# TensorE's K loop gets an empty first turn, and the MLP and q's products run at its end

## The chip, the cores and the metric

The kernel runs on one core of a Trainium2 chip. The metric is the device time of one execution in microseconds, the median of several runs. Four compute engines matter here: TensorE (PE, with PEld for its weight loads), VectorE (DVE), ScalarE (ACT) and GpSimd (POOL). SyncE (SP) issues nearly all DMAs, in the order of one queue.

## The reference

One decode step: sliding-window attention over a KV cache, an MLP with a shifting step, and their sum.

```python
def _A_ref(x, k_cache, v_cache, wq, wo):      # x (4,1,576), caches (4,16,8192,128)
    q = (x @ wq) ...                           # 32 heads of 128, two per KV head
    k = jnp.repeat(k_cache[:, :, Sk - W:, :], rep, axis=1)     # W = 2048
    v = jnp.repeat(v_cache[:, :, Sk - W:, :], rep, axis=1)
    p = _softmax(einsum("bhqd,bhkd->bhqk", q, k) * Dh ** -0.5)
    return einsum("bhqk,bhkd->bhqd", p, v) ... @ wo
def _B_ref(x, w1, w2, w3, w4):                 # 576 -> 576 -> 576 -> 4608 -> 576
    h = _gelu(_layernorm(x) @ w1)
    x1 = x + shifted(h) @ w2
    return x1 + _gelu(_layernorm(x1) @ w3) @ w4
xn = _layernorm(x)
return x + _A_ref(xn, ...) + _B_ref(xn, ...)
```

All data are bf16. The cache windows are 33.6 MB of K and as much of V; with the weights 88.49 MB are read from HBM.

## The kernel before

**Loads.** SP issues in this order: w1, w2, wq, w3, K load 0 in two halves, K loads 1 to 7, V loads 0 to 7 (the last in two halves), w4, wo in five pieces. A K or V load is 4,096 KB. K rotates through three slots (`kslot`), so from load 3 on a K load waits for the end of the transposes of the load three before it (`t_done`, semaphore `T`). K load 1 waits for q's products, K load 2 and the first V load for the products with w3. V loads 1 to 3 wait for transposes of the last K loads, V loads from 4 on for PV products, w4 and wo for later ones. Since all of these stand in one queue of issues, a waiting issue holds back those behind it.

**TensorE's prologue** (`prog["pe"]`, put out by `emit_program("pe", "pe", e)`). It runs before the loop: a zeroing product into q's bank, transposes of the normalised x (L328), nine products with w1 (L389), eighteen with w2 (L397), transposes of the third layer norm's output, 36 products with wq (L361), four transposes of q, two zeroing products, 72 products with w3 (L422), 18 products that transpose the MLP's hidden state (L435), and a wait for `Qs0`, the copy of q into the score groups' weights. In all 175 matmuls, each with its weight load.

**TensorE's K loop** (`nc.Fori`, L654). Eight turns, one for each K load, TensorE alone; the other engines have their programs unrolled. One turn has two halves `h`. A half transposes 64 blocks of 128x128 (`emit_T`, L474, into four PSUM banks in rotation), then multiplies one score group of 32 matmuls (`emit_SC`, L481) from the half before. The transposed blocks are evicted into `ktb` by VectorE (L462, five of eight) and ScalarE (L461, three of eight). Since the slot of a K load has to be a constant in the code, each half has three arms (`half(h, 0)`, `half(h, 1)`, `half(h, 2)`) and a register, `k_at`, chooses among them (L669 to L674). `turn` is the value that the loop's semaphore waits compare with: 1 in the first turn, 8 in the last.

**After it.** The last score group, softmax, a second loop for the PV products (L551), then the products with w4 and wo into one PSUM bank, and the result's DMA.

The order in which TensorE's instructions lie in memory is that of the code: prologue (361 instructions with the weight loads), loop (923), the rest (981).

## Time and profile before

| | |
|---|---|
| median of 3 runs | 219.47 us (218.48 to 220.06) |
| profiled execution | 218.1 us |
| its span, first to last instruction | 216.8 us |
| mean granted TensorE clock | 0.937 |
| PE busy | 179.4 us (83%) |
| DVE, ACT, POOL busy | 118.2, 61.5, 13.8 us |
| data read from HBM | 88.49 MB, 408 GB/s over the span |

How to read it: a busy TensorE is not one at its peak, as matmuls are pipelined and their ends are modelled. The DMA share says how much of the time the 16 DMA engines had packets, not how fast these went; the rate stands beside it. "Issue" as the reason of an idle time means that the engine waited for nothing that the profile shows. Branches and register steps of a sequencer are not counted as busy; they show up in the view of one source line.

### The profile page before, as it was taken

The page shows a single profiled execution, that of the slowest core. Times are in us where ns is not written, and L with a number is a line of the kernel's source. Part 1 is how long each engine was busy: PE and PEld are TensorE (multiplying, and loading weights), DVE is VectorE, ACT ScalarE, POOL GpSimd, SP SyncE. Part 2 cuts the span into 40 slices and gives each one's busy share as a digit, 9 for nine tenths or more (in the row PEclk, how much of TensorE's full clock was granted, in tenths as well). Part 3 has the DMA queues.
Part 4 walks back from the last instruction along what each step waited for, and adds up shares of the span by engine and source line. Part 5 has one row for each costly group of instructions (what it writes and reads, how often), then busy time and mean ns, then how long its engine had stood idle before and what let it go on. Part 6 is the DMA issues. An engine that isn't in the chain of part 4 may idle for free.

```text
span 216.8 us, 5426 instructions
## 1 busy us (share of the span) xinstructions
PE 179.4 (83%) x2459; PEld 144.3 (67%) x2459; DVE 118.2 (55%) x170; ACT 61.5 (28%) x69; POOL 13.8 (6%) x29
## 2 busy tenths in 40 slices
PE   1466254675999999999999996699999899999875
PEld 0222123655898888888888884489888698887442
DVE  5434201322677777787878784999966566401100
ACT  2003101131466656566555576400000000000000
POOL 8960000000000000000000000000000000000000
PEclk9995558767999999999999999999999999999999
DMA  7999899999999999999999999999999999999992
GB/s 268 413 435 490 367 428 423 426 475 393 404 423 378 399 387 405 411 435 387 441 431 429 441 417 447 423 438 357 411 426 435 435 426 411 459 445 429 388 414 106
DMA packets 4059, 88.66 MB, mean 409 GB/s; under 512 B 456, under 2 KB 592, under 8 KB 1104
## 3 DMA queue, kind: packets, MB, share of 16 engines
q1 hardware_dynamic: 4032, 88.49, 96.8%
q8 instruction: 9, 0.15, 0.3%
q14 instruction: 2, 0.02, 0.0%
q10 hardware_dynamic: 16, 0.01, 0.0%
HBM read 88.49 MB, written 0.00 MB: 408 GB/s over the span
## 4 chain that ended last, share of the span: by engine, by line
PE 61%; DMA 25%; DVE 5%; issue 5%; ACT 1%; SPq 1%; DVEq 0%
PE ps L474 27%; PE ps L551 20%; DMA vring<-in_A_wo_dram 13%; DMA vring<-in_B_w_dram 13%; PE ps L481 10%; PE ps L422 2%; SPq L200 1%; DVE rm L497 1%; DVE vring L494 1%; DVE ktb L543 1%; PE ps L511 1%; DVE ktb L462 1%; ACT Qpad L503 1%; ACT kring L527 1%; PE ps L562 0%
## 5 line engine op out<-in xcount | busy, mean ns | idle before, releaser
L461 ACT ACTIVATE ktb<-ps 128x1024 bf16<-128x1024 bf16 x48 | 49.3, 1027 | 45.4 <-PE ps L474 45.4
L462 DVE COPY ktb<-ps 128x1024 bf16<-128x1024 bf16 x80 | 52.1, 687 | 17.6 <-PE ps L474 16.6
L474 PE MATMUL ps<-ident_bf,kring 128*128 128x128 bf16 x768 | 49.1, 228 | 9.2 <-issue 8.6
L474 PEld LDWEIGHTS ps<-ident_bf,kring 128*128 128x128 bf16 x768 | 46.6, 102 | 13.2 <-issue 12.6
L543 DVE TENSOR_TENSOR ktb<-kring,mH_bf 128x4096 bf16<-128x4096 bf16 x16 | 36.2, 2290 | 10.1 <-PE ps L551 9.9
L551 PE MATMUL ps<-vring,ktb 128*128 128x256 bf16 x256 | 28.6, 273 | 3.0 <-DVE ktb L543 1.9
L551 PEld LDWEIGHTS ps<-vring,ktb 128*128 128x128 bf16 x256 | 24.9, 98 | 6.3 <-issue 3.5
L551 PE MATMUL ps<-kring,ktb 128*128 128x256 bf16 x256 | 28.6, 273 | 0.0
L551 PEld LDWEIGHTS ps<-kring,ktb 128*128 128x128 bf16 x256 | 25.0, 98 | 3.3
L481 PE MATMUL ps<-ktb,kring 128*32 128x256 bf16 x544 | 23.4, 315 | 0.1
L609 ACT ACTIVATE out_sb<-ps 4x288 bf16<-4x288 f32 x1 | 0.4, 399 | 75.8 <-PE ps L384 75.8
L481 PEld LDWEIGHTS ps<-ktb,kring 128*32 128x32 bf16 x544 | 14.3, 101 | 5.3 <-issue 0.8
L474 PE MATMUL ps<-ident_bf,vring 128*128 128x128 bf16 x256 | 15.2, 219 | 0.1
L474 PEld LDWEIGHTS ps<-ident_bf,vring 128*128 128x128 bf16 x256 | 14.3, 98 | 1.4 <-issue 1.1
L422 PE MATMUL ps<-vring,xs 128*8 128x320 bf16 (+1 forms) x72 | 4.5, 429 | 5.7 <-DMA vring<-in_B_w_dram 5.7
L492 DVE COPY vring<-ps 128x256 f32<-128x256 f32 x8 | 4.8, 605 | 7.4 <-PE ps L481 7.4
L494 DVE TENSOR_TENSOR vring<-vring,ps 128x256 f32<-128x256 f32 x8 | 5.4, 680 | 6.2 <-PE ps L481 6.2
L572 DVE TENSOR_SCALAR tmp<-ps,maskd 128x128 f32<-128x128 f32 x2 | 0.7, 352 | 13.7 <-PE ps L551 13.7
L328 PE MATMUL ps<-ident_bf,xp_bf 4*128 4x4 bf16 x15 | 0.8, 164 | 8.2 <-DVE xp_bf L312 5.0
L422 PEld LDWEIGHTS ps<-vring,xs 128*8 128x8 bf16 x72 | 2.1, 111 | 8.1 <-DMA vring<-in_B_w_dram 6.3
L610 DVE CAST out_sb<-ps 4x288 bf16<-4x288 f32 x1 | 0.4, 449 | 12.9 <-PE ps L384 12.9
L239 POOL MEMSET ktb<- 128x8192 bf16 x1 | 6.9, 6924 | 0.0
(93 smaller groups left out, 92.0 us busy)
## 6 DMA issues: line engine op xcount, KB each, us to landing
kring<-in_A_k_cache_dram SPq DMA_DIRECT2D x5, 4096.0 KB, 14.7
vring<-in_A_v_cache_dram SPq DMA_DIRECT2D x4, 4096.0 KB, 20.6
kring<-in_A_v_cache_dram SPq DMA_DIRECT2D x3, 4096.0 KB, 23.0
vring<-in_B_w_dram SPq DMA_DIRECT2D x2, 5184.0 KB, 23.2
vring<-in_A_k_cache_dram SPq DMA_DIRECT2D x2, 4096.0 KB, 20.2
kring<-in_A_wq_dram SPq DMA_DIRECT2D x1, 4608.0 KB, 15.6
kring<-in_A_k_cache_dram SPq DMA_DIRECT2D x2, 2048.0 KB, 35.1
kring<-in_A_v_cache_dram SPq DMA_DIRECT2D x2, 2048.0 KB, 19.3
```

What stands on the lines that cost most here:

```text
L200: e.dma_start(o_, i_).then_inc(S[skey], 16)
L239: P(lambda e: e.memset(ktb[:, NKT // 2 * 1024:NKT * 1024], 0.0), key=-92, inc=(("E", LB - 2), 1))
L422: ins = e.matmul(H2ps[k][32 * j:32 * j + 2 * B].rearrange("b (p t) -> b p t", t=n), lhsT=x_at(2, s_), rhs=w[:, :, 9 * j + t0:9 * j + t0 + ...
L461: return "act", lambda e: e.activation(out=ktbuf[:, n % NKT], in_=tb[n % 4], func=ACTF.Copy)
L462: return "dve", lambda e: e.tensor_copy(out=ktbuf[:, n % NKT], in_=tb[n % 4])
L474: ins = e.transpose(tb[j % 4][:, t, :], kslot(k)[:, Dh * (8 * j + t):Dh * (8 * j + t + 1)], ident_bf[:])
L481: ins = e.matmul(ps[32 * u:32 * u + 32, k, 0:256].rearrange("p (t i) -> p t i", t=NT), lhsT=Qs[:, 32 * h:32 * h + 32], rhs=ktgrp[:, k, :, ...
L492: add("dve", lambda e, c=c: e.tensor_copy(out=S_at(c), in_=R_at(c)), waits=w, key=key)
L494: add("dve", lambda e, c=c: e.tensor_tensor(out=S_at(c), in0=S_at(c), in1=R_at(c), op=ALU.add), waits=w, sig="S_last" if last else f"S{c}" ...
L497: add("dve", lambda e, c=c: e.tensor_reduce(out=rm4[:, c % 8 // 2:c % 8 // 2 + 1], in_=S_sb[:, c % 8 // 2, :], axis=AX.X, op=ALU.max), wai ...
L543: return lambda e: e.tensor_tensor(out=PTpad[:, n % 4], in0=PTv[:, qt, NH * h:NH * (h + 1), bp, :].unsqueeze(2).to_broadcast([128, NH, NX, ...
L551: ins = e.matmul(ps[:, 0, 0:256], lhsT=PTpad[:, 2 * (k % 2) + h, 2 * g:2 * g + 2].rearrange("p t h e -> p (t h e)"), rhs=slot(k)[:, Dh * t ...
```

## The change

The loop gets one turn more, and the prologue moves from ahead of the loop into it, at the end of a turn and under a condition. In the added first turn `k_at` is 0: every arm and both score groups are passed over, and the prologue runs. In the eight turns behind it `k_at` is 32, 64 or 96, chooses the arm as 0, 32 and 64 did before, and the prologue is passed over. `turn` is 0 in the added turn and 1 to 8 in the others, as before. Arms and score groups, and the programs of the other engines, are the same.

```diff
         e = nc.tensor
-        emit_program("pe", "pe", e)
-        with nc.Fori(0, N_LOOP, engines=[PE]) as it:
-            turn = e.snap(it + 1)
-            k_at = e.snap(it * 32 - ((it * 11) & 96) * NKS, min_val=0, max_val=64)
+        with nc.Fori(0, 1 + N_LOOP, engines=[PE]) as it:
+            turn = e.snap(it + 0)
+            k_at = e.snap(((it + 7) & 8) * 12 + (it + 2) * 32 - (((it + 2) * 11) & 96) * NKS - 64, min_val=0, max_val=96)
...
             for h in range(2):
-                with e.If(k_at > 32):
+                with e.If(k_at > 64):
                     half(h, 2)
                 with e.Else():
-                    with e.If(k_at > 0):
+                    with e.If(k_at > 32):
                         half(h, 1)
                     with e.Else():
-                        half(h, 0)
+                        with e.If(k_at > 0):
+                            half(h, 0)
                 k = 1 - h
-                for x in (6, 7):
-                    e.wait_ge(S["E", NBLK * k + x], turn)
-                emit_SC(e, k).then_inc(S["SC"], 1)
+                with e.If(k_at > 0):
+                    for x in (6, 7):
+                        e.wait_ge(S["E", NBLK * k + x], turn)
+                    emit_SC(e, k).then_inc(S["SC"], 1)
+            with e.If(k_at < 1):
+                emit_program("pe", "pe", e)
```

In the program that comes of it, TensorE's code has 2,271 instructions for 2,265. The loop begins at instruction 4 instead of 361 and ends at 1,290 instead of 1,284; the prologue's 358 instructions are its last part.

## The prediction

> **What bounds the kernel now.** I read the page first: span, DMA queues, instruction queue.

> ```profile
> span 216.8 us, 5426 instructions
> ...
> q1 hardware_dynamic: 4032, 88.49, 96.8%
> q8 instruction: 9, 0.15, 0.3%
> ```

> The data queue is occupied for 96.8% of the span, so the end is set by 88.49 MB of loads. What can still be won is the rate inside that share. A table of stretches shows it:

> ```profile
> core 0: us, PE busy (x) PEld busy (x) DVE busy (x) ACT busy (x) POOL busy (x), PEclk, DMA share, GB/s
> 50.00:111.00 61.00, 58.82 (x1095) 52.31 (x1096) 44.30 (x71) 34.92 (x34) 0.00 (x0) 0.97 0.98 406
> 111.00:141.00 30.00, 25.92 (x432) 20.47 (x429) 22.57 (x36) 18.12 (x22) 0.00 (x0) 1.00 1.00 433
> 141.00:162.00 21.00, 21.00 (x191) 18.44 (x189) 18.60 (x11) 0.00 (x0) 0.00 (x0) 1.00 0.99 407
> ```

> In both slow stretches the share is nearly full and the rate 6% lower than between them, although from 111 to 131 the same K loop with the same evictions runs. So neither engine traffic nor the memory itself explains the 6%. What differs is how early the next load is queued. SP's issues and the times from issue to landing:

> ```profile
> 34.19 0.54 SPq L200 DMA_DIRECT2D vring<-in_A_k_cache_dram  x1
> 56.43 11.07 SPq L200 DMA_DIRECT2D kring<-in_A_k_cache_dram  x2
> ...
> 117.86 10.93 SPq L200 DMA_DIRECT2D kring<-in_A_v_cache_dram  x2
> 147.19 0.54 SPq L200 DMA_DIRECT2D vring<-in_A_v_cache_dram  x1
> ```

> ```profile
> vring<-in_A_k_cache_dram SPq DMA_DIRECT2D x1, 4096.0 KB, 25.9
> ```

> ```profile
> kring<-in_A_k_cache_dram SPq DMA_DIRECT2D x5, 4096.0 KB, 14.7
> ...
> kring<-in_A_v_cache_dram SPq DMA_DIRECT2D x3, 4096.0 KB, 23.0
> ```

> K load 2 (issued at 34.19, the single row of 25.9 to landing) lands at 60.1; load 3 is issued at 56.43, so it joins the queue 3.7 us before the queue runs dry. The later K loads land 14.7 us after issue; a 4.19 MB load at 406 GB/s takes 10.3, so their lead is about 4.4. V load 3 (the second issue of the row at 117.86, about 128.3, and 23.0) lands at 151.3, and V load 4 is issued at 147.19: lead 4.1. V loads with 23.0 from issue to landing have a lead of some 13, and their stretch has 433 GB/s. My reading: with a lead near 4 us some of the 16 DMA engines run out before the next load reaches them, with a longer one they don't. Full rate in the first slow stretch would save 61 x (1 - 406/433) = 3.8 us, in the second 21 x (1 - 407/433) = 1.3.

> The lead is set by TensorE: a K load waits until the transposes of three turns earlier have freed its slot. So why is TensorE late?

> ```profile
> 1.38 0.61 PE L352 MATMUL ps<-zeros_bf 128*128 128x512 bf16 x1 [1.38 <-POOL zeros_bf L233]
> ...
> 8.50 2.32 PE L389 MATMUL ps<-ktb,xs 128*8 128x288 bf16 x9 [0.78 <-DVE xs L334]
> ...
> 29.65 4.49 PE L422 MATMUL ps<-vring,xs 128*8 128x320 bf16 x72 [5.74 <-DMA vring<-in_B_w_dram]
> 34.63 0.79 PE L435 MATMUL ps<-ident_bf,h_sb 128*64 128x16 bf16 x18 [0.49 <-ACT h_sb L441]
> 37.66 3.90 PE L474 MATMUL ps<-ident_bf,kring 128*128 128x128 bf16 x38 [2.25 <-issue]
> 43.46 2.05 PE L474 MATMUL ps<-ident_bf,kring 128*128 128x128 bf16 x26 [1.91 <-issue]
> 45.44 1.90 PE L481 MATMUL ps<-ktb,kring 128*32 128x256 bf16 x32
> 51.04 5.36 PE L474 MATMUL ps<-ident_bf,kring 128*128 128x128 bf16 x64 [3.70 <-issue]
> 56.33 1.73 PE L481 MATMUL ps<-ktb,kring 128*32 128x256 bf16 x32
> 58.25 0.94 PE L474 MATMUL ps<-ident_bf,kring 128*128 128x128 bf16 x14 [0.20 <-issue]
> ```

> Then the branches of two lines, and the instruction fetches between 60 and 130 us:

> ```profile
> L669 PEldq COMPARE_BRANCH  x20: 68/208/457, 36.6 to 123.1; - x20
> ```

> ```profile
> L672 PEldq COMPARE_BRANCH  x18: 70/169/4923, 37.1 to 127.5; - x18
> ```

> ```profile
> q8 instruction: 1, 0.02, 0.1%
> ```

> The first turn of the K loop takes 20.6 us (37.66 to 58.25). Inside it TensorE stands still for 1.91 and 3.70 us with nothing to wait for but its own sequencer, and one branch lasts 4,923 ns where the usual one lasts 169. The page counts nine instruction fetches of 0.15 MB / 9 = 16 KB in the whole span; the last row, of the stretch from 60 to 130 us, counts one. So the first turn pays for code that TensorE has not yet, and the other seven find it there.

> **The change, part by part.** The program order shows the loop's code moved ahead of the MLP and of q, which now stand at its end behind a branch. Turn 0 jumps over six arms and two score groups, then runs the old prologue. All code of the loop lies between turn 0's first and last instruction, so its blocks are fetched then.

> *Added at the start.* At 16 KB a block and 2,271 TensorE instructions in some nine or ten blocks, a block is about 256 instructions. The skipped arms are 926 instructions, the prologue 358: turn 0 needs about two blocks that weren't loaded beforehand on its way to the first matmul, one more within the first MLP products, and one that has most of the prologue to arrive. Price of each: 1.9 us (the stall at 43.46) to 4.9 (the long branch). I take 3.5, between the ends, since at 1 us hardly a load is queued ahead: first matmul near 8.4 instead of 1.38, the group of 8.50 at about 9.3, and its end some 4 us later with its own fetch. What follows moves with it, q and the issue of K load 1 too; but w3 (landed at 29.6) and K load 0 stand ahead of that in the queue until about 40, so its issue has more than 10 us to spare. The cover for the rest is the 5.74 us in which TensorE waits for w3 ahead of 29.65, and w3's load does not depend on TensorE. So 0; without that cover, 4.

> *Removed in the first real turn.* Of the 2.25 us ahead of 37.66 the sequencer's way through the loop's head gets about 0.25 longer (more steps, priced below): start at 37.9. Then 64 transposes without the 1.91 stall, a score group, 64 transposes without the 3.70: 5.6 us less. Part of the old first turn ran at half clock (64 transposes in 5.36 us, later 3.68), and an unbroken run may shed that earlier or later: bounds -1.5 and +1.7, taken 1.0 in favour. The last transposes of this turn end near 50.0 instead of 56.4, and the next turn starts near 52.0 instead of 58.25. K load 1 permits it: it lands one load ahead of load 2's 60.1, near 50. TensorE is then 6.2 us ahead of before.

> *Added in every turn.* The way around the loop, in the chain of waits:

> ```profile
> 73.12 3.68 PE ps L474 x64
> 76.80 1.27 PE ps L481 x23
> 78.07 0.28 issue
> ```

> The sequencer passes the loop's head while the 1.27 us of the score group run, and here the head is 0.28 too long. The cover is used up, so what is added is paid: one taken branch over the prologue (208 ns), one untaken ahead of the second score group (68), in one arm another, one register step more; with about 0.06 between instructions 0.43 to 0.66 by arm. Bounds 0.35 (nothing between) and 0.8 (four steps at 208). The untaken branch ahead of the first score group hides under 64 transposes (3.68 us, over which the sequencer is ahead): 0, or 0.13 a turn without that. Six more trips around: 6 x 0.54 = 3.2 of the 6.2 us are given back. The last score groups end 3.0 us earlier, and softmax and PV after them.

> *What the lead buys.* K loads 3 to 7 are then issued with a lead of 60.1 - 50.0 = 10 us, falling by about 0.9 a turn (a turn of 10.6 against 9.7 for a load at 433 GB/s) to 6.5. What a lead between 4.4 and 13 is worth, V load 5 shows:

> ```profile
> vring<-in_A_v_cache_dram SPq DMA_DIRECT2D x1, 4096.0 KB, 14.9
> ```

> ```profile
> 154.35 0.54 SPq L200 DMA_DIRECT2D vring<-in_A_v_cache_dram  x1
> ```

> ```profile
> vring<-in_A_v_cache_dram SPq DMA_DIRECT2D x1, 4096.0 KB, 17.4
> ```

> V load 4 lands at 147.19 + 14.9 = 162.1, so load 5 at 154.35 had a lead of 7.7, and it landed at 171.8, 9.7 after load 4: full rate. Bounds for the first slow stretch are 0 and 3.8; I take nine tenths, 3.4, as the leads are nearer to 7.7 than to 4.4. V load 4 is issued 3.0 earlier against a queue that ends 3.4 earlier: its lead stays near 4, and of the 1.3 there I count 0 (bounds -0.4 and 1.3). Sum: 3.4. Span 216.8 - 3.4 = 213.4. The profiled execution took 218.1 in all (1.3 around its span), so 214.7; the median of the runs, 219.47, stands 1.4 above it: 216.1, and I write 216.0.

> [...]

> **The rivals.**

> *The lead buys nothing* (the K loads' 406 GB/s has another cause, or TensorE loses its lead at the upper bound of 0.8 us a trip, 4.8 in six, after a first turn that gains only 4). For it: the share already reads 0.98. Against: 433 GB/s under the same loop from 111 to 131. Time: 219.5, or up to 2 less.

> *The start is not covered* (slower). If each block costs 4.9, the first matmul is at 11.2, the first MLP group ends about 8.4 later, and if the fourth block isn't ahead either, 13 later in all, of which 5.74 are hidden. The transposes then start up to 7.3 late. It decides from 5.74 + 3.0 = 8.7 us of added delay: beyond that the K loop ends later than before, and every lead of 4.4 shrinks, V load 4's by all of 4.1. At 13 us TensorE is some 4 late at the end; six thin leads cost 3.8 + 1.3 = 5.1 now, 0.85 each, and I price the thinner ones at 0.7 more: about 223.7. Against it: at 1 us nothing else is in the queue, and later blocks can be asked for ahead.

> *The loop's code doesn't fit* (slower, and the change then does not do what it says). The loop spanned 923 instructions and now spans 1,286, one or two blocks more; the trace of before can't show that they stay. If blocks are lost, six come again in each turn at 1.9 us of standstill or more: 8 x 6 x 1.9 = 91 us, less the lead: about 300.

> **How the numbers follow.** The forecast has 0.64, nothing gained 0.20, the start not covered 0.11, the code not fitting 0.05. A measurement of this kernel can tell about 1% (2.2 us). Of the forecast's cases nearly all gain more (its own range 214.0 to 217.5): faster 0.63, within 1% 0.22, slower 0.15. The range is 214.0 (the transposes warm early, V load 4 covered too: 5.1 won, with the median's spread) to 219.8 (nothing gained).

> **What would show it.** Right: instruction fetches of TensorE's queue within the first 15 us and none in the first real turn; first matmul near 8; the products with w3 still at about 29.7 behind w3's load; transposes starting near 38 without idle time over 1 us; turns of 10.5 instead of 10.0; issue of K load 3 near 50; 425 GB/s or more from 50 to 111. Wrong: L422 starting after 31; fetches in every turn; K loads landing 10.2 apart in spite of leads over 6 us.

## The result and the profile after

The changed kernel takes 217.5 us (median of 20 runs, 215.55 to 219.97), the kernel before 219.35 in the same comparison: ratio 0.9909, interval 0.9881 to 0.9937. It is faster by 0.9%, 1.9 us, where 3.4 was forecast. The profiled execution (219.05 us) is one of four slow ones among the 20, which the ratio leaves out; its last products ran at half clock (0.52 granted from 213.65 to 216 us), so its span is not compared below, only its stretches.

Page of the changed kernel:

```profile
span 217.8 us, 5473 instructions
...
q1 hardware_dynamic: 4032, 88.49, 95.5%
q8 instruction: 9, 0.15, 0.3%
```

As many code fetches as before, and as many bytes. Its stretches, to be set against those of before:

```profile
core 0: us, PE busy (x) PEld busy (x) DVE busy (x) ACT busy (x) POOL busy (x), PEclk, DMA share, GB/s
50.00:111.00 61.00, 57.06 (x1099) 50.44 (x1097) 44.93 (x72) 35.80 (x35) 0.00 (x0) 1.00 1.00 426
111.00:141.00 30.00, 25.42 (x416) 19.87 (x413) 22.10 (x35) 17.17 (x22) 0.00 (x0) 1.00 1.01 434
141.00:162.00 21.00, 21.00 (x191) 18.44 (x190) 18.60 (x9) 0.00 (x0) 0.00 (x0) 1.00 0.93 384
```

The K stretch (50 to 111 us) rose from 406 to 426 GB/s. The V stretch (141 to 162) fell from 407 to 384, and there the DMA share fell too, from 0.99 to 0.93. In time: 61 x (1 - 406/426) = 2.9 us won, 21 x (1 - 384/407) = 1.2 lost, 1.7 in all.

That is near the 1.9 us between the medians, but it is not the whole account of this execution, which took 0.95 us more than the profiled one of before. By the landings of the loads it is 0.2 us behind at K load 2 (60.34 for 60.10) and 1.1 us ahead at the end of V load 7 (190.19 for 191.26). Then w4 lands 13.95 us later, where it was 12.27 before, although it was issued 6.4 us before the queue ran dry, much as before (6.7). What costs these 1.7 us is open. One other profile has them at a long lead (13.80 us at 7.4, in the kernel before with q's products moved, see below), so they don't come of the change alone.

TensorE's instructions in order of time show where the gain and the loss come from:

```profile
15.81 0.60 PE L352 MATMUL ps<-zeros_bf 128*128 128x512 bf16 x1 [15.81 <-issue]
...
17.50 1.60 PE L389 MATMUL ps<-ktb,xs 128*8 128x288 bf16 x6 [0.73 <-DVE xs L334]
20.67 0.88 PE L389 MATMUL ps<-ktb,xs 128*8 128x288 bf16 x3 [1.57 <-issue]
...
34.76 3.46 PE L422 MATMUL ps<-vring,xs 128*8 128x320 bf16 x72
38.71 0.79 PE L435 MATMUL ps<-ident_bf,h_sb 128*64 128x16 bf16 x18 [0.48 <-ACT h_sb L441]
42.25 5.36 PE L474 MATMUL ps<-ident_bf,kring 128*128 128x128 bf16 x64 [2.75 <-issue]
47.54 1.34 PE L481 MATMUL ps<-ktb,kring 128*32 128x256 bf16 x32
48.81 3.75 PE L474 MATMUL ps<-ident_bf,kring 128*128 128x128 bf16 x64
52.49 1.33 PE L481 MATMUL ps<-ktb,kring 128*32 128x256 bf16 x32
54.47 1.72 PE L474 MATMUL ps<-ident_bf,kring 128*128 128x128 bf16 x28 [0.65 <-issue]
```

The first real turn takes 12.2 us (42.25 to 54.47) instead of 20.6, with no standstill inside. But it starts 4.6 us later. The first matmul is at 15.81 instead of 1.38, and the products with w3 at 34.76 no longer wait for w3 at all, so the 5.74 us of cover are used up and 5.1 us stick out. Two branches of the empty turn, the maxima of these rows, hold 12.1 of the 14.4 us by which the first matmul is later (minimum, median and maximum in ns):

```profile
L677 PEldq COMPARE_BRANCH  x18: 65/65/5742, 2.6 to 127.0; - x18
```

```profile
L671 PEldq COMPARE_BRANCH  x20: 65/169/6378, 2.0 to 126.7; - x20
```

And the way around the loop. The kernel before had 0.28 us of idle time in the arm of the prediction's view, and 0.14 and none in the other two:

```profile
87.02 1.26 PE ps L481 x28
88.28 0.14 issue
88.42 3.73 PE ps L474 x64
...
97.11 1.25 PE ps L481 x25
98.36 3.68 PE ps L474 x64
```

The changed kernel has 0.91 and 0.65 in the first two of these arms:

```profile
73.42 1.26 PE ps L481 x26
74.68 0.91 issue
75.59 3.73 PE ps L474 x64
79.32 1.26 PE ps L481 x30
80.58 3.68 PE ps L474 x64
84.26 1.26 PE ps L481 x26
85.52 0.65 issue
```

Its third arm has 0.34. The last score groups end at 130.0, 0.7 us earlier than before. What that makes of the leads (how long before the landing of the load ahead a load is issued):

```profile
38.27 0.54 SPq L200 DMA_DIRECT2D vring<-in_A_k_cache_dram  x1
52.59 11.12 SPq L200 DMA_DIRECT2D kring<-in_A_k_cache_dram  x2
...
116.62 11.43 SPq L200 DMA_DIRECT2D kring<-in_A_v_cache_dram  x2
146.49 0.54 SPq L200 DMA_DIRECT2D vring<-in_A_v_cache_dram  x1
```

```profile
kring<-in_A_k_cache_dram SPq DMA_DIRECT2D x5, 4096.0 KB, 16.6
```

K load 2 lands at 60.3 (22.1 after its issue), K load 3 is issued at 52.59: a lead of 7.7 instead of 3.7. The K loads land 16.6 us after issue instead of 14.7, of which 9.8 are transfer at 426 GB/s: lead 6.8 instead of 4.4. Load by load, the leads fall from 7.7 us at K load 3 to 4.3 at K load 7. The first four of these five land 9.7 us after the load ahead, the last one 10.8; before, with leads of 3.3 to 4.7, it was 9.9 to 11.3. V load 3, the second issue of the row at 116.62 (127.5), takes 21.3 and lands at 148.8. V load 4 comes at 146.49 with a lead of 2.3 instead of 4.1, since the queue ahead of it ends 2.5 us earlier and TensorE only 0.7; it lands 12.2 us after V load 3 instead of 10.8.

### The profile page after: what moved, and what is told of

Read it like the earlier page. It is cut to its first block, busy times and chain, and to the rows that moved or that the text cites. A ratio compares the mean times of both kernels' runs of the same rounds, so it can differ in the third digit from the quotient of the medians.

```text
span 217.8 us, 5473 instructions
## 1 busy us (share of the span) xinstructions
PE 176.1 (81%) x2459; PEld 141.9 (65%) x2459; DVE 118.3 (54%) x170; ACT 61.5 (28%) x69; POOL 13.8 (6%) x29
## 3 DMA queue, kind: packets, MB, share of 16 engines
q1 hardware_dynamic: 4032, 88.49, 95.5%
HBM read 88.49 MB, written 0.00 MB: 406 GB/s over the span
## 4 chain that ended last, share of the span: by engine, by line
PE 65%; DMA 13%; DVE 7%; POOL 6%; issue 5%; ACT 2%; SPq 1%; POOLq 0%; DVEq 0%
PE ps L474 26%; PE ps L551 19%; DMA vring<-in_A_wo_dram 13%; PE ps L481 10%; POOL ktb L239 3%; PE ps L397 2%; PE ps L361 2%; PE ps L422 2%; DVE rm L497 1%; PE ps L389 1%; DVE vring L494 1%; PE ps L384 1%; DVE ktb L543 1%; PE ps L511 1%; DVE ktb L462 1%
## 5 line engine op out<-in xcount | busy, mean ns | idle before, releaser
L474 PE MATMUL ps<-ident_bf,kring 128*128 128x128 bf16 x768 | 46.9, 223 | 6.8 <-issue 6.5
L474 PEld LDWEIGHTS ps<-ident_bf,kring 128*128 128x128 bf16 x768 | 44.6, 100 | 10.5 <-issue 9.9
L481 PE MATMUL ps<-ktb,kring 128*32 128x256 bf16 x544 | 22.6, 311 | 0.0
L481 PEld LDWEIGHTS ps<-ktb,kring 128*32 128x32 bf16 x544 | 13.8, 100 | 4.9 <-issue 0.3
L474 PE MATMUL ps<-ident_bf,vring 128*128 128x128 bf16 x256 | 15.1, 219 | 0.8 <-issue 0.7
L474 PEld LDWEIGHTS ps<-ident_bf,vring 128*128 128x128 bf16 x256 | 14.3, 98 | 2.2 <-issue 1.9
L352 PE MATMUL ps<-zeros_bf 128*128 128x512 bf16 (+2 forms) x3 | 1.0, 392 | 15.8 <-issue 15.8
L352 PEld LDWEIGHTS ps<-zeros_bf 128*128 128x128 bf16 x3 | 0.3, 101 | 15.8 <-issue 15.8
L610 DVE CAST out_sb<-ps 4x288 bf16<-4x288 f32 x1 | 0.4, 448 | 14.7 <-PE ps L384 14.7
L308 ACT ACTIVATE sd<-mv 4x1 f32<-4x1 f32 x3 | 0.6, 202 | 24.9 <-DVE mv L306 24.9
## 6 DMA issues: line engine op xcount, KB each, us to landing
kring<-in_A_k_cache_dram SPq DMA_DIRECT2D x5, 4096.0 KB, 16.6
vring<-in_A_v_cache_dram SPq DMA_DIRECT2D x4, 4096.0 KB, 20.5
kring<-in_A_v_cache_dram SPq DMA_DIRECT2D x3, 4096.0 KB, 21.3
vring<-in_A_k_cache_dram SPq DMA_DIRECT2D x2, 4096.0 KB, 19.0
kring<-in_A_k_cache_dram SPq DMA_DIRECT2D x2, 2048.0 KB, 34.8
```

The costliest lines, as they stand in the source:

```text
L474: ins = e.transpose(tb[j % 4][:, t, :], kslot(k)[:, Dh * (8 * j + t):Dh * (8 * j + t + 1)], ident_bf[:])
L481: ins = e.matmul(ps[32 * u:32 * u + 32, k, 0:256].rearrange("p (t i) -> p t i", t=NT), lhsT=Qs[:, 32 * h:32 * h + 32], rhs=ktgrp[:, k, :, ...
```

## The experiments

Theory A: the rate of the loads follows from how early the next one is queued, and that from where TensorE stands. Theory B: TensorE's place does not matter, and the 6% between the stretches have another cause. The stretch tables have the columns of the one above.

**The branches alone** (`turn` and `k_at` start at the values of the changed kernel's turn 1)

```diff
-        with nc.Fori(0, 1 + N_LOOP, engines=[PE]) as it:
...
+        emit_program("pe", "pe", e)
+        with nc.Fori(0, N_LOOP, engines=[PE]) as it:
...
             with e.If(k_at < 1):
-                emit_program("pe", "pe", e)
+                pe_idle(8)(e)
```

> The change's branches alone: the MLP and q's products stand ahead of the loop as before, there is no empty first turn, but every turn passes the added branches (in place of the prologue a few matmuls that never run are jumped over). Theory A (the rate of the loads follows from how early the next one is queued, and that from where TensorE stands): first turn as before, still with its two standstills; then 0.35 to 0.6 us more idle time at each trip around, the K loop ends about 3.5 us later than before (near 134), the leads of the K loads fall from about 4 us to 1 to 2, the rate from 50 to 111 us under 400 GB/s; time 222 to 225, ratio 1.013 to 1.025. Theory B (TensorE's place does not matter, the 6% between the stretches has another cause): 219.4, ratio 1.00.

Measured: 222.53 us, ratio 1.0158 (1.0118 to 1.0198). Its stretches:

```profile
50.00:111.00 61.00, 54.98 (x1012) 49.03 (x1013) 41.17 (x65) 32.26 (x32) 0.00 (x0) 0.95 0.93 376
111.00:141.00 30.00, 26.25 (x482) 21.56 (x480) 20.54 (x34) 17.79 (x22) 0.00 (x0) 1.00 1.01 435
141.00:162.00 21.00, 19.07 (x175) 16.21 (x173) 20.34 (x14) 2.97 (x4) 0.00 (x0) 1.00 0.93 386
```

TensorE fell back further than expected: the first turn with its standstills took 22.4 us (20.6 before), and the last score groups start at 134.0 instead of 128.2. The two outer stretches, whose loads wait for a late TensorE, fall to 376 and 386 GB/s; between them 435 stays. Theory B in this form falls. Without the empty turn the branches cost 1.6%, of which the longer first turn is a part; that the changed kernel is faster in spite of them is the work of the empty turn.

**q's products ahead of the third norm's transposes**

```diff
-            add("pe", pe_xT(2), waits=["ln3"], sig="xT2", key=-37)
+            add("pe", pe_xT(2), waits=["ln3"], sig="xT2", key=-29)
```

> The changed kernel with one group moved: q's 36 products ahead of the five transposes of the third layer norm's output, so that they run in the 3 us in which TensorE waits for that norm. Theory A: the products with w3 start near 31.2 instead of 34.8, the first transposes near 38.7 instead of 42.25, the K loop ends near 126.5 instead of 130.1; leads 3.5 us longer; rate from 50 to 111 near 433, from 141 to 162 over 410; time about 215, ratio 0.98. Theory B: as the changed kernel, ratio 0.991.

Measured: 214.62 us, ratio 0.9808 (0.9775 to 0.9841). The group with w3 waits for w3 again:

```profile
31.11 4.28 PE L422 MATMUL ps<-vring,xs 128*8 128x320 bf16 x72 [0.57 <-DMA vring<-in_B_w_dram]
35.87 0.79 PE L435 MATMUL ps<-ident_bf,h_sb 128*64 128x16 bf16 x18 [0.49 <-ACT h_sb L441]
39.42 6.44 PE L474 MATMUL ps<-ident_bf,kring 128*128 128x128 bf16 x64 [2.76 <-issue]
```

3.65 us earlier at w3, 2.8 at the transposes, and the rates are 432 and 414 GB/s for 426 and 384. So the late start cost the changed kernel about 1%. V load 4 still has a lead of only 3.2 us and lands 11.0 us after V load 3. The same edit on the kernel before:

> The kernel before with q's 36 products ahead of the third norm's transposes. If that move pays in the changed kernel only because its start is late against w3's load, it does nothing here: the products with w3 still start at 29.7 behind w3's landing, ratio 1.00 (0.997 to 1.003). If it pays by itself (rival): ratio 0.99.

Measured: 219.05 us, ratio 0.9964 (0.9933 to 0.9996). The products with w3 start at 29.71 in it, as before. The ratio lies just under the 0.997 to 1.003 that were expected, and the interval just under 1: a gain of at most 0.7%, less than the 1.0% that the edit is worth in the changed kernel.

**The prologue in the innermost Else**

```diff
                         with e.If(k_at > 0):
                             half(h, 0)
+                        if h == 1:
+                            with e.Else():
+                                emit_program("pe", "pe", e)
...
-            with e.If(k_at < 1):
-                emit_program("pe", "pe", e)
```

> The changed kernel with the prologue inside the innermost Else of the second half, so that real turns need no taken branch over it. Start as in the changed kernel (first matmul near 15.8, first transposes near 42.2). Idle time ahead of a turn falls by about 0.27 us, to 0.38, 0.07 and 0.64 by arm, so that the K loop ends near 128.2. Theory A: time about 216.3, ratio 0.986. Theory B: ratio 0.991.

Measured: 214.87 us, ratio 0.9847 (0.9805 to 0.9889). The chain of waits:

```profile
71.83 1.27 PE ps L481 x30
73.10 0.63 issue
73.73 3.73 PE ps L474 x64
77.47 1.26 PE ps L481 x29
78.73 3.68 PE ps L474 x64
82.41 1.25 PE ps L481 x25
83.66 0.34 issue
```

0.63 for 0.91 and 0.34 for 0.65: the taken branch over the prologue costs 0.28 and 0.31 us, near the 0.27 that were priced. The transposes also start 1.85 us earlier (40.40), which was not expected. The standstill of 1.57 us inside the products with w1 is gone: the code fetch behind it came at 18.45 us in the changed kernel, here it comes at 19.72 and TensorE does not stand still. The score group that lay between the arms and the prologue is behind it now, which shifts the blocks' ends; that this is the reason is likely, but no run tests it. How the gain of this kernel divides between the shorter way around and the earlier start is open.

**Both edits**

> Both edits: q's products ahead of the third norm's transposes, and the prologue in the innermost Else. Theory A: first transposes near 38.7, K loop ends near 124.7, all leads over 5 us, time about 214, ratio 0.976. Theory B: ratio 0.991.

Measured: 213.92 us, ratio 0.9788 (0.9756 to 0.982). The first transposes start at 40.04 and the K loop ends at 126.0, both 1.3 us later than expected.

> The kernel with both edits on the changed one once more, beside the others on the same chip: ratio 0.976 to 0.982.

Measured: 213.69 us, ratio 0.9762 (0.9716 to 0.9808): the lowest median here, and clearly ahead of the kernel before and of the changed one.

**K loads in halves, TensorE as before**

```diff
-            for n, (u0, u1) in enumerate([(0, NH), (NH, NTV)] if c == 0 else [(0, NTV)]):
+            for n, (u0, u1) in enumerate([(0, NH), (NH, NTV)] if c == 0 or c >= NKS else [(0, NTV)]):
+                if c >= NKS and n == 0:
+                    w = [f"T{2 * NBLK * (c - NKS) + NBLK - 1}"]
+                elif c >= NKS:
+                    w = [t_done(c - NKS)]
...
```

> The kernel before with K loads 3 to 7 in two halves, the first issued when the first half of the slot is transposed (some 5 us earlier than now); TensorE's program is that of before. Theory A (the lead of a load sets the rate): leads of the K loads rise from about 4 to about 9 us with no change on TensorE, the rate from 50 to 111 us rises from 406 to about 430, the K loop still ends near 130.7; V load 4's lead falls by the same 3 us to about 1, and 141 to 162 falls under 390. Time 216.5 to 218, ratio 0.987 to 0.994, about what the change itself gave. Theory B (the K loads' rate rises only where TensorE's fetches or its standstills are gone): 406 GB/s and ratio 1.00.

Measured: 217.61 us, ratio 0.9918 (0.9883 to 0.9952), the changed kernel's gain without any of its edits.

```profile
50.00:111.00 61.00, 59.39 (x1114) 52.88 (x1113) 45.26 (x72) 35.74 (x35) 0.00 (x0) 0.98 1.01 428
111.00:141.00 30.00, 25.73 (x420) 20.29 (x419) 22.61 (x35) 17.29 (x22) 0.00 (x0) 1.00 1.00 428
141.00:162.00 21.00, 20.95 (x190) 18.45 (x190) 18.60 (x9) 0.00 (x0) 0.00 (x0) 1.00 0.94 389
```

406 became 428 and 407 became 389, with TensorE's standstills still in place:

```profile
42.15 2.75 PE L478 MATMUL ps<-ident_bf,kring 128*128 128x128 bf16 x26 [2.67 <-issue]
...
49.73 5.11 PE L478 MATMUL ps<-ident_bf,kring 128*128 128x128 bf16 x64 [3.27 <-issue]
```

So theory B of this run falls too. The halves from K load 3 on have leads of 8.3 us or more and land 4.9 to 5.1 us after the one ahead. Two halves thus take no less time than one whole load with a long lead (9.7 us), so the early issue is enough to account for the gain; whether smaller pieces also bear a thin lead better is not shown. V load 4's lead is 1.9 us here. V loads in halves as well:

> The kernel before, TensorE's K loop and prologue untouched, with K loads 3 to 7 and the V loads in halves, so that a half is issued as soon as its half of the slot is free. Theory A: the K loads keep a lead over 6 us, V load 4 gets one of about 5, both stretches run at 425 GB/s or more; time 214.5 to 216, ratio 0.98, better than the changed kernel with none of its edits. Theory B (TensorE must be earlier): ratio not under 0.99.

Measured: 216.61 us, ratio 0.9874 (0.9816 to 0.9933). The rates are 425 and 418 GB/s, so 2.7 + 0.6 us won; the forecast had counted on more. The trace shows a new thin lead at w4: it is issued 2.7 us before the queue runs dry (6.7 before) and lands 13.9 us after the last V load (12.3 before). A simple change to the loads gives about as much as the empty turn gave; the two intervals overlap.

**The price of a fetch.** The change with one wait added, SyncE's first load behind TensorE's first matmul:

```diff
-        ev_w1 = add_dma([(w1_t, runs(B_w1))], "w1", (), -50)
+        ev_w1 = add_dma([(w1_t, runs(B_w1))], "w1", ["q_zero"], -50)
```

> The changed kernel with SyncE's first load held back until TensorE's first matmul is done, so that the code fetches of the empty turn meet no data packets. Theory A (a fetch's price is mostly waiting among the data packets of the DMA engines): the two long branches fall from 5.7 and 6.4 us to 2 to 3 each, the first matmul is at 7 to 9 us. Theory B (the price is the fetch's own): they stay over 5 us, first matmul near 15. The time says nothing here: loads start later by that much.

Measured: the same two branches take

```profile
L677 PEldq COMPARE_BRANCH  x18: 65/65/3141, 2.6 to 134.4; - x18
```

```profile
L671 PEldq COMPARE_BRANCH  x20: 65/169/3041, 2.0 to 134.2; - x20
```

3.0 and 3.1 us are the fetch's own price; the other 3.3 and 2.6 us of the changed kernel are waiting among data packets. The traces show the wait: one packet of 16 KB belongs to each of the two branches, it takes 1.0 to 1.3 us in both kernels, and it begins 0.9 and 0.4 us after the start of its branch here, where the DMA engines are all but idle (5 GB/s over the first 10 us), and 3.4 and 4.1 us after it in the changed kernel. The first matmul that the trace keeps is at 10.42, where 7 to 9 was expected. (224.43 us in its one run, as the loads start late.)

**V loads in halves on top of both edits**

> The kernel with both earlier edits (q's products ahead, prologue in the innermost Else), and V loads in halves, so that V load 4's first half is issued after the first half of its slot's PV products, 3.5 us earlier. Theory A: its lead rises from about 3 to 6.5 us, the rate from 141 to 162 from 414 to about 430, time about 213, ratio 0.974. If the lead there is worth nothing: 213.9, ratio 0.979.

Measured: 214.01 us, ratio 0.9741 (0.9703 to 0.9778).

> Both edits and V loads in halves once more, on the same chip: if V load 4's lead still cost time in the kernel with both edits, 0.4 to 1.0 us below it (ratio about 0.975); if not, the same.

Measured: 214.03 us, ratio 0.9762 (0.9716 to 0.9808), beside 0.9762 for both edits alone. No gain can be seen, although V load 4's first half now has a lead of 9.5 and 8.3 us in the two profiles and lands 4.9 us after the load ahead, 9.8 for two halves. In the kernel with both edits V load 4 had a lead of 3.8 us in one profile (10.7 us after V load 3, and 414 GB/s from 141 to 162) and 5.4 in the other (9.7 us, 433 GB/s). In the first TensorE's granted clock was 0.94 from 111 to 141 us, for 1.00 in the second, and its first 64 PV products took 8.82 us instead of 7.16. So there is about 1 us to win here in one execution and nothing in another; the medians don't resolve it.

## Why the prediction was right, and where it was off

*What bounds the kernel: right.* A lead near 4 us costs rate, a longer one does not. The DMA share shows it where one load follows another: 0.85 (344 GB/s) from 59 to 61 us in the kernel before, at a lead of 3.7 us, for 1.10 (475) in the changed one, at 7.7; and 0.66 (221) in the changed kernel from 146 to 150, at 2.3. Across the profiles the K stretch has 376 GB/s with TensorE later than before, 406 before, 415 with q's products moved in the kernel before, 426 with the change, 427 to 432 with the start mended, and 425 and 428 with longer leads alone. Load by load it is sharper. In the eleven profiles whose K loads 3 to 7 are whole, all 40 of these loads with a lead of 5.2 us or more landed 9.7 us after the load ahead. The 15 with a lead of 5.0 us or less took 9.7 to 12.8 us, 13 of them at least 9.9. V load 4, where it is whole, took 10.4 to 12.2 us at leads of 1.9 to 4.3 and 9.7 at 5.4. The V stretch falls when the K stretch rises and TensorE doesn't follow (384, 389).

*The start: the step that failed.* "I take 3.5, between the ends, since at 1 us hardly a load is queued ahead." The two blocks cost 5.7 and 6.4 us, over the upper bound of 4.9, and the first matmul came at 15.8 for 8.4. The empty turn reaches its first missing block at 2.6 us. By then the loads issued since 0.8 fill the DMA engines (a share of 1.03 from 2 to 16 us); the fetches are 3.0 and 3.1 us where they don't. That later blocks can be asked for ahead shows elsewhere: in the kernel before, the fetch at 54.3 us begins within the transposes of 51.04, and the score group behind them starts at 56.33 without idle time. Without the cover everything behind would have been 5.1 + 5.74 = 10.8 us late, for the 4 that were counted. By the prediction's own sign (L422 starting after 31) this step was wrong. So the second rival came true by half: 5.1 us stuck out. Its point of decision, 8.7 us, was passed, and yet the K loop ended no later than before, because the next step was worth more than I gave it.

*The first real turn: right, and undersized.* It took 8.4 us less than before (12.2 for 20.6), where 6.6 had been counted. The two standstills are 5.6 of that. The other 2.8 stood in the forecast with 1.0 and a bound of 1.7: the unbroken turn had a clock of 0.68 in its first half and 1.00 after it, and its transposes took 5.36 and 3.75 us, where the two halves before had 5.95 and 5.36 of work.

*The trips around the loop: right.* 0.65, 0.34 and 0.91 for 0.14, 0 and 0.28 is 0.34 to 0.63 more; six trips make 3.0 us where 3.2 had stood.

*The lead's worth: right for K, off for V.* TensorE ended 0.7 us ahead of before, not 3.0. The K leads fell 0.9 us a turn, as worked out, but from 7.7 and not from 10, so that K load 7 was thin again; the K stretch won 2.9 us of the 3.4 forecast. V load 4's lead fell to 2.3 instead of staying near 4, and its stretch lost 1.2 us where the bound was 0.4. The edit that takes 3.65 us off the start gives 214.6, which is 1.4 under the forecast.

*The number: partly luck.* The time lies within the range, with 1.9 us gained for 3.4. But two errors met in it: a start that delayed TensorE by 10.8 us for 4, and a first real turn that saved 1.8 us more than was counted.

*The code: it stays.* There are nine fetches of 16 KB, as before, five of them ahead of 41 us. From 41 to 130 us, in eight turns of a loop of 1,286 instructions, none is of that queue (q8; the next is at 143.7):

```profile
q1 hardware_dynamic: 1308, 38.14, 100.2%
q14 instruction: 2, 0.02, 0.0%
```

Each of the two long branches, 5.7 and 6.4 us, has one of the fetches in it (at 6.08 and 12.79 us). The block of about 256 instructions was an estimate from nine fetches for 2,271 instructions (252 each). No run shows how many instructions a fetch brings, and in the kernel before all nine come from 33.8 us on, when most of the prologue has run.

## What to carry to other kernels

When the DMA queue is busy all the time, look at its rate by stretch: a stretch that runs 6% slower at a full share may be one whose next load is queued only 4 us ahead, and a split load that is issued when half of its slot is free can mend that without touching the compute (406 GB/s became 428 here). Fetching a loop's code ahead of time pays in full only where the fetches themselves are covered (here 5.74 us of cover met 10.8 us of delay), so ask what else the DMA engines are doing at that moment, and check which work has slack there. When one part of a queue gets faster, the next load whose issue nobody moved gets a thinner lead, as V load 4 did here (2.3 us for 4.1), and w4 in the kernel with K and V loads in halves (2.7 for 6.7).
